# Sums over V ahead of both units' scores at the head of an even turn

## The chip, the cores and the metric

The kernel runs on one core of a Trainium2 chip. The metric is the device time of one execution in microseconds (us). TensorE (PE) multiplies matrices, VectorE (DVE), ScalarE (ACT) and GpSimd (POOL) work on elements, and SyncE (SP) issues the transfers. Each engine runs its instructions in the order in which the program lists them; between engines they wait for one another by semaphores.

## The reference

Top-k attention over 8 batches, 8 heads, 576 positions and a head width of 64, then a SwiGLU feed-forward block over the 4608 resulting rows of 512 (inner width 1536). In short:

```
scores = q @ k.T / 8                              # 576 x 576 for each batch and head
kth    = 32nd largest score of each row
attn   = softmax(scores where scores >= kth, else -1e9)
x      = (attn @ v), heads put side by side        # 4608 x 512
out    = (silu(x @ w_gate) * (x @ w_val)) @ w_out  # 4608 x 512
```

All of it is fp32.

## The kernel before, in words

**Units.** Attention is cut into units of one batch, one block of 128 query rows (`qt`) and one pair of heads (`hp`): 576 rows make four blocks of 128 and one of 64. A unit of a block of 128 is a full unit: two heads, 576 scores each for 128 rows. The last block of a batch gives half units: its 64 rows of both heads lie together on 128 partitions. A batch has 16 full units and then 4 half units; there are 160 units in all.

**Turns.** The main loop (L843) makes one turn for each unit `n`. The loop's body fixes the order of work by hand, and the end of the kernel (L912 to L925) ties each engine's instructions to that order. In turn `n`:

- VectorE selects the top 32 of unit `n` (`select`, L322: four rounds of MAX8, L334, with three MATCH_REPLACE8, L338, for each head).
- ScalarE turns unit `n-1` into exponentials (`weigh`, L354: a Prelu, L361, and an Exp with its sum, L366, for each head). From unit 32 on VectorE adds a small constant to the sums (L379), and it takes their reciprocals (L380, `normalize`). ScalarE (L384) and GpSimd (L386) then scale the two heads.
- TensorE transposes unit `n-2` (`turn`, L390: into PSUM tiles `etps`, L400), and ScalarE copies the result into the tile `et` (L401).
- At an even turn TensorE multiplies the transposed weights of units `n-4` and `n-3` by V (`values`, L411: 40 matmul records, L434, into one PSUM tile `av`), and ScalarE copies these sums into `xT`, the input of the feed-forward block (L450). That is "the sums over V of two units". `finish_units` (L820) calls this, and at the end of a batch's units it also starts the load of the next batch's V (`load_v`, L237).
- At an even turn TensorE makes the scores of units `n+1` and `n+2` (`scores`, L284). For a full unit these are four products into four PSUM tiles `s` (L314, eight records), each of which ScalarE copies with its scale into `sc` (L319); for a half unit two tiles (L300, L305). The generator stops once between the matmuls and the copies, so that a caller can place these apart. The second unit's copies come only after `weigh`, since the three buffers of `sc` allow no more.
- The feed-forward block runs in pieces in between (`piece`, L751; `feed`, L564): products with the weights (tile `f`, L578), gates on ScalarE and GpSimd (L611 to L619) and the output products (`y_ps` and `x_ps`, L644). A planner gives each turn a credit (`share`, L787), from the costs of its other work, and takes pieces while it lasts: two right after the head of the turn, one or two later, the rest at the end of the turn. Work that ScalarE and GpSimd still owe to pieces is put into two lists (`on_act`, `on_pool`) and written out at fixed places (`flush`).
- Now and then a turn also prepares keys and queries of a later pair of heads (`fetch`, `prep`: transposes into `kqps`, L267 and L260, and copies L263, L264 and L272).

**Buffers.** PSUM is in two pools: `ps_t` with five tiles (scores, `av`, `etps`, `kqps`), given out one after the other in a circle, and `ps_f` with three (products of the feed-forward block). A tile can be written again when the copy that reads its last contents is done.

**The place of the change** is the head of the turn:

```python
        flush(on_pool)
        if nxt:
            run(nxt.pop(0))           # scores of unit n+1, with their copies
        if valued(n):
            finish_units(valued(n))   # sums over V of units n-4 and n-3
        if nxt:
            next(nxt[0])              # matmuls of unit n+2's scores
        early[0]()
        if 0 <= n - 1 < NU:
            weigh(n - 1)
        if nxt:
            run(nxt.pop())            # copies of unit n+2's scores
```

Here `scored(n)` (L801) names the units to score: both at an even turn, none at an odd one (turns 0 and 1 score one each). `valued(n)` (L806) names the two units to sum, at even turns only.

Of the kernel before, what the change touches and what calls it, by code (L numbers as in the profile page):

```python
# [25 lines left out]
def kernel(  # L26
# [174 lines left out]
    def rounding(n):  # L201
        for _ in range(n):
            next(weight, None)
# [33 lines left out]
    def load_v(i):  # L237
        b, hp = pairs[i]
        h = slice(2 * hp, 2 * hp + 2)
        vt = slabs.tile([P, 2, J, D], FP32, tag="v", name="v")  # L240
        v_last = slabs.tile([R, 2, D], FP32, tag="vl", name="v_last")
        vl = vlast[i % NV]
        nc.sync.dma_start(
            vt[:].rearrange("p h j d -> p h (j d)"),
            v[b, h, 0:JP].rearrange("h (p j) d -> p h (j d)", j=J),
        )
        nc.sync.dma_start(v_last[:], v[b, h, JP:S].rearrange("h p d -> p h d"))
        for hh in range(2):
            o = hh * R
            nc.sync.dma_start(vl[o : o + R, o : o + R], v[b, 2 * hp + hh, JP:S])  # L250
        vs[i] = (vt, v_last, vl)
# [28 lines left out]
    def n_heads(qt):  # L280

        return 1 if qt == J else 2

    def scores(n):  # L284
        b, qt, hp = units[n]
        slab = preps[b * NHP + hp]
        sc = work.tile([P, 2 * S], FP32, tag="sc", name="sc", bufs=3)
        halves = [slice(0, D), slice(D, P)]
        half = S // 2

        def bank():
            return ps_t.tile([P, 512], FP32, tag="t", name="s")


        if qt == J:
            banks = [bank() for _ in range(2)]
            for i, ps in enumerate(banks):
                for d in halves:
                    k0 = R + i * half
                    nc.tensor.matmul(  # L300
                        ps[d, 0:half], slab[d, S + R : S + 2 * R], slab[d, k0 : k0 + half]
                    )
            yield
            for i, ps in enumerate(banks):
                nc.scalar.mul(sc[:, i * half : (i + 1) * half], ps[:, 0:half], scale)  # L305
        else:
            q0 = S + 2 * R + qt * P
            banks = []
            for i in range(2):
                for hh, d in enumerate(halves):  # L310
                    ps = bank()
                    banks.append((i + 2 * hh, ps))
                    k0 = (1 - hh) * R + i * half
                    nc.tensor.matmul(  # L314
                        ps[:, 0:half], slab[d, q0 : q0 + P], slab[d, k0 : k0 + half]
                    )
            yield
            for i, ps in banks:
                nc.scalar.mul(sc[:, i * half : (i + 1) * half], ps[:, 0:half], scale)  # L319
        state[n] = dict(sc=sc)  # L320

    def select(n):  # L322

        nh = n_heads(units[n][1])
        sc = state[n]["sc"]
        m = small.tile([P, 2, TOP_K], FP32, tag="m", name="m")
        heads = [slice(t * S, (t + 1) * S) for t in range(nh)]
        e = work.tile([P, 2 * S], FP32, tag="e", name="e", bufs=3)
        state[n] |= dict(m=m, e=e, heads=heads)
        cur = sc  # L330
        rounds = TOP_K // 8
        for r in range(rounds):
            for t, hs in enumerate(heads):
                nc.vector.max(m[:, t, 8 * r : 8 * r + 8], cur[:, hs])  # L334
                yield
            if r < rounds - 1:
                for t, hs in enumerate(heads):
                    nc.vector.match_replace(  # L338
                        e[:, hs], m[:, t, 8 * r : 8 * r + 8], cur[:, hs], LOWEST
                    )  # L340
                    yield
                cur = e

    def shift(n):

        st = state[n]
        m, nh = st["m"], len(st["heads"])
        bias = small.tile([P, 2], FP32, tag="bias", name="bias")
        nc.gpsimd.tensor_tensor(  # L349
            bias[:, 0:nh], m[:, 0:nh, TOP_K - 1], m[:, 0:nh, 0], ALU.subtract  # L350
        )
        st["bias"] = bias
# [21 lines left out]
    def normalize(n):  # L374
        st = state[n]
        tot, e, heads = st.pop("tot"), st["e"], st.pop("heads")
        nh = len(heads)
        for t in range(nh if n >= AHEAD else 0):
            nc.vector.tensor_scalar_add(tot[:, t : t + 1], tot[:, t : t + 1], EPS)  # L379
        nc.vector.reciprocal(tot[:, 0:nh], tot[:, 0:nh])  # L380
        yield
        for t, hs in enumerate(heads):
            if t == 0 and n >= 3 * NHP:
                nc.scalar.mul(e[:, hs], e[:, hs], tot[:, t : t + 1])  # L384
            else:
                nc.gpsimd.tensor_tensor(  # L386
                    e[:, hs], e[:, hs], tot[:, t : t + 1].to_broadcast([P, S]), ALU.mult
                )
# [83 lines left out]
    def flush(queue):  # L472
        while queue:
            queue.pop(0)()
# [303 lines left out]
    def fetch(n):  # L778

        b, qt, hp = units[n]  # L780
        i = b * NHP + hp
        if qt == 0:
            yield from prep(i)
        if qt == J and i + NHP < len(pairs):
            load(i + NHP)

    def share(n):  # L787


        others = 0.0  # L790
        costs = [(m, 0.7) for m in scored(n) + valued(n)] + [(n - TURN, 0.6)]
        for m, cost in costs:
            if m >= 0:
                others += cost * (0.5 if units[m][1] == J else 1)
        if units[n + 3][1] == 0:
            others += 0.6

        beside = 5.8 if n < AHEAD else 6.4
        return beside * n_heads(units[n][1]) / 2 - others

    def scored(n):  # L801

        ahead = [n + 1] if n < 2 else [] if n % 2 else [n + 1, n + 2]
        return [m for m in ahead if m < NU]

    def valued(n):  # L806

        behind = [] if n % 2 else [n - 4, n - 3]
        return [m for m in behind if 0 <= m < NU]

    def pieces(n):
        for _ in range(n):
            if credit[0] >= 1:
                credit[0] -= piece()

    def run(steps):
        for _ in steps:
            pass

    def finish_units(ns):  # L820
        values(ns)
        for n in ns:
            b, qt, hp = units[n]
            if qt == J and b + 1 < B:
                load_v((b + 1) * NHP + hp)
# [17 lines left out]
    for n in range(NU + 3):  # L843
        nh = n_heads(units[n][1]) if n < NU else 1
        topk = select(n) if n < NU else no
        norm = normalize(n - 1) if 0 <= n - 1 < NU else no
        nxt = [scores(m) for m in scored(n)]
        ahead = fetch(n + 3 if n else 2) if n + 3 < NU else no

        def dve(k, beside=True):  # L850

            for _ in range(k * nh):
                next(topk, None)
                due[0] += 5 / 6 if beside else 0
                if due[0] >= 1:
                    due[0] -= 1
                    rounding(1)

        if n >= NU - NHP:
            credit[0] = 8.0  # L860
        else:
            credit[0] = min(credit[0] + share(n), share(n) + 1)
        flush(on_act)
        if 0 <= n - 1 < NU:
            shift(n - 1)
        flush(on_pool)
        if nxt:
            run(nxt.pop(0))
        if valued(n):
            finish_units(valued(n))  # L870
        if nxt:
            next(nxt[0])
        early[0]()
# [3 lines that stand above are left out]
            run(nxt.pop())  # L877


        dve(2, beside=False)  # L880
        if n == 0:
            run(ahead)
            load(3)
            ahead = fetch(3)
        if n < NHP:
            load_v(n)
        pieces(2)
        flush(on_act)
        dve(1)
        dve(1)  # L890
        if 0 <= n - TURN < NU:
            run(turn(n - TURN))

        flush(on_pool)
        next(ahead, None)
        pieces(1)
        next(ahead, None)
        dve(1)
        pieces(1)
        if n < AHEAD:  # L900
            dve(1, beside=False)
        run(norm)
        dve(1 if n < AHEAD else 2, beside=False)
        run(topk)
        pieces(6)
# [50 lines left out]
```

## Time and profile before

| what | us |
|---|---|
| median of 3 runs | 1760.57 |
| lowest, highest run | 1758.68, 1762.17 |
| the profiled execution | 1759.77 |
| its span, first to last instruction | 1758.0 |
| TensorE busy in the span | 1679.6 |
| VectorE busy | 1476.5 |
| ScalarE busy | 1262.3 |
| GpSimd busy | 798.8 |

The mean granted clock of TensorE was 0.974 of full speed. Times in a timeline count from the span's start. A row of a timeline stands for consecutive records of one kind: start, length, engine, line, operation, output from inputs, shapes, their number, and in brackets how long the engine was idle before and what ended that. PE stands for matmuls, PEld for the loading of weights, which overlaps them. Matmuls are pipelined and their ends are modelled, so the distance between starts tells more than the ends do. The attention part ends at about 1690 us; after that only feed-forward work is left.

### The profile page before, as it was taken

What the parts mean: (1) busy time and instruction counts of PE and PEld (TensorE: products, weight loads), DVE (VectorE), ACT (ScalarE), POOL (GpSimd) and SP (SyncE); (2) the same over time, 40 slices, a digit from 0 to 9 for tenths busy, and PEclk for the clock granted to TensorE, in tenths of its full rate; (3) what the DMA queues carried; (4) which work ended last, traced back from release to release, by engine and by line L of the source; (5) the groups of instructions that cost most, each with busy time, mean ns of one, the idle gap of its engine ahead of it and who ended that gap; (6) DMA issues with size and microseconds to landing.
All of it is one profiled execution on the core that took longest, in us unless ns stands there. A gap on an engine that the chain in (4) does not pass through costs nothing.

```text
span 1758.0 us, 31754 instructions
## 1 busy us (share of the span) xinstructions
PE 1679.6 (96%) x11408; PEld 1404.5 (80%) x11408; DVE 1476.5 (84%) x3311; ACT 1262.3 (72%) x2901; POOL 798.8 (45%) x910
## 2 busy tenths in 40 slices
PE   5578999999999999999999999999999999999999
PEld 3468588787888788887888878887888878788887
DVE  6999899989889899898899898898988988898300
ACT  7899787777767686768776777777776777676431
POOL 4898534343353425352535334443444433535434
PEclk6698999999999999999999999999999999999999
DMA  7442120003000120002100020000300020000000
GB/s 200 138 120 86 29 68 1 13 2 83 15 13 1 28 70 1 13 12 59 28 13 1 14 70 27 1 13 19 78 2 13 1 57 15 13 1 13 1 13 12
DMA packets 109309, 59.72 MB, mean 34 GB/s; under 512 B 88544, under 2 KB 96992, under 8 KB 109152
## 3 DMA queue, kind: packets, MB, share of 16 engines
q1 hardware_dynamic: 108016, 57.37, 12.5%
q8 instruction: 90, 1.47, 0.4%
q14 instruction: 67, 0.55, 0.1%
q10 hardware_dynamic: 1136, 0.33, 0.1%
HBM read 48.23 MB, written 9.44 MB: 33 GB/s over the span
## 4 chain that ended last, share of the span: by engine, by line
PE 81%; DVE 8%; ACT 8%; POOL 1%; issue 1%; DMA 1%; SPq 0%; ACTq 0%; POOLq 0%
PE f L578 37%; PE av L434 9%; PE x_ps L644 9%; PE s L314 7%; PE y_ps L644 7%; PE etps L400 6%; DVE m L334 4%; DVE e L338 3%; PE f L494 3%; ACT e L366 2%; PE s L300 2%; PE kqps L267 1%; ACT e L361 1%; ACT et L401 1%; PE o_ps L546 1%
## 5 line engine op out<-in xcount | busy, mean ns | idle before, releaser
L334 DVE MAX8 m<-e 128x8 f32<-128x576 f32 x864 | 615.0, 748 | 3.1
L338 DVE MATCH_REPLACE8 e<-m,e 128x576 f32<-128x576 f32 x576 | 423.9, 743 | 0.0
L578 PE MATMUL f<-xT,wg 128*128 128x256 f32 x1536 | 355.0, 381 | 0.0
L578 PE MATMUL f<-xT,wv 128*128 128x256 f32 x1536 | 353.9, 380 | 0.0
L578 PEld LDWEIGHTS f<-xT,wg 128*128 128x128 f32 x1536 | 287.7, 190 | 45.7 <-issue 8.4
L578 PEld LDWEIGHTS f<-xT,wv 128*128 128x128 f32 x1536 | 286.8, 190 | 42.7 <-issue 5.5
L614 POOL TENSOR_TENSOR h<-h,half_g 128x512 f32<-128x512 f32 x96 | 122.5, 1276 | 352.7 <-ACT h L613 336.8
L366 ACT ACTIVATE e<-e,bias 128x576 f32<-128x576 f32 x288 | 221.2, 776 | 34.1 <-POOL bias L349 30.9
L400 PE MATMUL etps<-ident,e 128*128 128x128 f32 (+1 forms) x1312 | 182.9, 281 | 46.7 <-POOL e L386 19.3
L400 PEld LDWEIGHTS etps<-ident,e 128*128 128x128 f32 (+1 forms) x1312 | 154.3, 143 | 76.9 <-POOL e L386 25.3
L338 DVE MATCH_REPLACE8 e<-m,sc 128x576 f32<-128x576 f32 x288 | 211.9, 742 | 0.0
L361 ACT ACTIVATE e<-sc,m 128x576 f32<-128x576 f32 x288 | 211.3, 786 | 0.0
L334 DVE MAX8 m<-sc 128x8 f32<-128x576 f32 x288 | 203.3, 743 | 7.5 <-ACT sc L319 7.5
L319 ACT ACTIVATE sc<-s 128x288 f32<-128x288 f32 x512 | 167.5, 414 | 53.4 <-PE s L314 53.0
L619 POOL TENSOR_TENSOR h<-h,val 128x512 f32<-128x512 f32 x96 | 122.5, 1276 | 178.5 <-ACT val L618 166.0
L386 POOL TENSOR_TENSOR e<-e,tot 128x576 f32<-128x576 f32 x140 | 160.8, 1152 | 87.4 <-DVE tot L380 76.2
L401 ACT COPY et<-etps 128x512 f32<-128x512 f32 (+1 forms) x448 | 183.4, 489 | 12.2 <-PE etps L400 11.7
L314 PE MATMUL s<-kqT 64*128 64x288 f32 x1024 | 171.3, 444 | 16.4 <-ACT et L401 8.3
L379 DVE TENSOR_SCALAR tot<-tot 128x1 f32<-128x1 f32 x228 | 29.4, 146 | 172.0 <-ACT e L366 171.9
L434 PE MATMUL av<-et,v 128*64 128x128 f32 (+1 forms) x2560 | 158.7, 267 | 0.0
L384 ACT ACTIVATE e<-e,tot 128x576 f32<-128x576 f32 x148 | 118.5, 801 | 46.5 <-DVE tot L380 46.2
L314 PEld LDWEIGHTS s<-kqT 64*128 64x128 f32 x1024 | 95.1, 191 | 62.2 <-issue 24.0
(85 smaller groups left out, 2279.0 us busy)
## 6 DMA issues: line engine op xcount, KB each, us to landing
v<-in_v_dram SPq DMA_DIRECT2D x32, 256.0 KB, 3.4
kq_in<-in_k_dram SPq DMA_DIRECT2D x63, 128.0 KB, 2.9
kq_in<-in_q_dram SPq DMA_DIRECT2D x63, 128.0 KB, 3.3
w<-in_moe_w_gate_dram SPq DMA_DIRECT2D x12, 512.0 KB, 3.9
w<-in_moe_w_val_dram SPq DMA_DIRECT2D x12, 512.0 KB, 3.7
w<-in_moe_w_out_dram SPq DMA_DIRECT2D x12, 512.0 KB, 3.6
out_dram<-o SPq DMA_DIRECT2D x38, 128.0 KB, 2.4
out_dram<-o SPq DMA_DIRECT2D x16, 256.0 KB, 2.4
```

What stands on the lines that cost most here:

```text
L314: nc.tensor.matmul(ps[:, 0:half], slab[d, q0 : q0 + P], slab[d, k0 : k0 + half])
L319: nc.scalar.mul(sc[:, i * half : (i + 1) * half], ps[:, 0:half], scale)
L334: nc.vector.max(m[:, t, 8 * r : 8 * r + 8], cur[:, hs])
L338: nc.vector.match_replace(e[:, hs], m[:, t, 8 * r : 8 * r + 8], cur[:, hs], LOWEST)
L361: nc.scalar.activation(e[:, hs], sc[:, hs], AF.Prelu, bias=m[:, t, TOP_K - 1 : TOP_K], scale=-1.0, alpha=SMALL,)
L366: nc.scalar.activation(e[:, hs], e[:, hs], AF.Exp, bias=bias[:, t : t + 1], scale=-1.0 / SMALL, accum_out=tot[:, t : t + 1],)
L386: nc.gpsimd.tensor_tensor(e[:, hs], e[:, hs], tot[:, t : t + 1].to_broadcast([P, S]), ALU.mult)
L400: nc.tensor.transpose(ps[0:kl, c * P : (c + 1) * P], e[:, k0 : k0 + kl], ident[:])
L401: nc.scalar.copy(et[0:kl, c0 : c0 + cn, :], ps[0:kl, 0 : cn * P].rearrange("p (c j) -> p c j", c=cn),)
L434: nc.tensor.matmul(av[d, i, 0:ql], weights_, moving, start=c == (0 if last else J), stop=c == (J if last else J - 1),)
L578: nc.tensor.matmul(ps[:, i, :], w[:, kc, m * P : (m + 1) * P], x[:, kc, :], start=(kc == 0), stop=(kc == KC - 1),)
L644: nc.tensor.matmul(ps, lhsT, T[i][m], start=m == 0, stop=m == MQ - 1)
```

## The change

At the head of a turn the two blocks change places: `finish_units` now comes ahead of the scores of unit `n+1`. On TensorE an even turn's head so has the 40 matmuls of `av` first and then the scores of both units, one after the other. On ScalarE the copy of `av` (L450) comes ahead of the four copies of unit `n+1`'s scores (L319). The PSUM tiles of `ps_t` are given out in that new order. Nothing is added or left out; odd turns and turns without both kinds of work keep their order.

```diff
@@ -864,10 +864,10 @@
         if 0 <= n - 1 < NU:
             shift(n - 1)
         flush(on_pool)
+        if valued(n):
+            finish_units(valued(n))
         if nxt:
             run(nxt.pop(0))
-        if valued(n):
-            finish_units(valued(n))
         if nxt:
             next(nxt[0])
         early[0]()
```

## The prediction

> **What bounds the kernel now.** I read the page first: its busy line, then windows by stage, to see where TensorE is full.
>
> ```profile
> PE 1679.6 (96%) x11408; PEld 1404.5 (80%) x11408; DVE 1476.5 (84%) x3311; ACT 1262.3 (72%) x2901; POOL 798.8 (45%) x910
> 0.00:200.00 200.00, 147.97 (x999) 114.85 (x999) 182.59 (x382) 167.36 (x373) 147.38 (x136) 0.81 0.43 121
> 400.00:1600.00 1200.00, 1189.18 (x8065) 998.76 (x8067) 1074.57 (x2450) 879.32 (x2032) 502.71 (x605) 1.00 0.10 24
> ```
>
> (Windows: stretch, length, busy us of PE, PEld, DVE, ACT, POOL, then clock and DMA.) From 400 to 1600 us TensorE is 99% busy at full clock, so its order of work sets the end; in the first 200 us it has slack and VectorE (91%) sets the pace. "Busy" hides short pauses between matmuls, and the change acts on exactly those. So I next asked who waits for whom.
>
> ```profile
> DVE tot L379 <- ACT e L366: 171.9, 107, 13.1
> PE etps L400 <- ACT sc L319: 19.3, 13, 3.9
> PE s L314 <- ACT et L401: 8.3, 3, 3.5
> PE s L314 <- ACT sc L319: 6.8, 3, 5.9
> ```
>
> (us, times, longest.) TensorE hardly waits; VectorE waits for ScalarE's exponentials 107 times, so it follows TensorE through ScalarE and has room. Last, the timeline of a head of an even turn with two full units, TensorE first, then ScalarE:
>
> ```profile
> 890.96 1.89 PE L578 MATMUL f<-xT,wg 128*128 128x256 f32 x8
> 892.78 1.24 PE L314 MATMUL s<-kqT 64*128 64x288 f32 x8
> 893.95 0.44 PE L434 MATMUL av<-et,vlast 128*64 128x128 f32 x4
> ...
> 896.29 1.24 PE L314 MATMUL s<-kqT 64*128 64x288 f32 x8
> 897.46 1.35 PE L578 MATMUL f<-xT,wg 128*128 128x256 f32 x5
> ...
> 893.57 1.32 ACT L319 ACTIVATE sc<-s 128x288 f32<-128x288 f32 x4 [1.82 <-PE s L314]
> 896.40 0.37 ACT L450 COPY xT<-av 128x256 f32<-128x256 f32 x1 [1.52 <-PE av L434]
> 896.67 1.45 ACT L361 ACTIVATE e<-sc,m 128x576 f32<-128x576 f32 x2
> ```
>
> By starts: first scores 1.17 us, sums over V 2.34, second scores 1.17; a head of 4.68 us from s to f. ScalarE stands idle before the scores' copies and again before the copy of the sums: it has room here.
>
> One place shows what scores cost when their banks come free one by one from ScalarE's copies:
>
> ```profile
> 348.63 1.33 ACT L319 ACTIVATE sc<-s 128x288 f32<-128x288 f32 x4
> 349.11 1.65 PE L314 MATMUL s<-kqT 64*128 64x288 f32 x8 [0.19 <-ACT sc L319]
> 350.69 0.48 PE L578 MATMUL f<-xT,wg 128*128 128x256 f32 x1
> ```
>
> There s to f is 1.58 us instead of 1.17. The four copies last 1.33 with single records of 0.43, so they follow each other at 0.30; the first ends at 349.06 and the matmul starts at 349.11, 0.05 later.
>
> **What the skill says.** The Trainium skill, "TensorEngine Tiling (Array Packing)", Key Properties: changing the tiling mode, not only the tile, drains TensorE. The trace agrees: s is 64\*128, av 128\*64, f 128\*128. Eight f take 1.82 us ahead of s (890.96 to 892.78), where eight at the pitch of 0.216 (24 of L578 in 5.18 in the chain) take 1.73: 0.09 to leave. Single records within the s row start 0.35, 0.24, 0.24 apart and the next row 0.34 after the last: 0.10 to enter, 0.10 to leave. "TensorE: Matmul & The Clock Gate", Part 3, The mechanism: matmuls start in program order, so one that waits for a bank holds what is behind it; the stretched s row at 349.11 fits that.
>
> **The change, part by part.** No instruction is added or removed. At an even turn the 40 matmuls of av and ScalarE's copy L450 go ahead of s of unit n+1; the second s row then follows the first directly.
>
> (a) *One change of mode less.* Before: f, s, av, s, f; after: f, av, s, s, f. The pair "out of av, into s" stays, "out of s, into av" goes: about 0.10 + 0.05 (first step in av 0.16 instead of 0.11), and "f to s" becomes "f to av", 0.05 cheaper. Gain 0.20 us a head if nothing waits.
>
> (b) *A wait for banks.* Tag t has five banks, given out in turn. Before, the order is s ABCD, av E, s ABCD, and 2.34 us of av cover the four copies that free A to D. After, it is av A, s BCDE, s ABCD: of the second row, bank 1 needs the copy of av, banks 2, 3, 4 the first three copies of the row just before, and no work lies between. With the sums first, s begins 2.33 after the head. The first copy starts 0.79 after it (893.57 minus 892.78), the third ends 0.79 + 2 x 0.29 + 0.42 = 1.79 after it, and its bank's matmul starts at 1.84 instead of 1.57. In the row at 349.11 the last bank was freed three copies after the first, at 0.90, and f came at 1.58: 0.68 later. So f follows at 1.84 + 0.68 = 2.52, and the head is 2.33 + 2.52 = 4.85 us against 4.68: **+0.17 net**, (a) included. ScalarE must be free by 2.4 for this; in every full head after 410 us its earlier work ends at most 2.0 after the head.
>
> (c) *How many.* I sorted the heads by time. After 410 us 42 have two full units ahead (FF): 36 of them at 4.68 (or 4.09, where the sums are of half units; after, 1.75 + 2.52 = 4.27): 36 x 0.17 = +6.1. The other six, first in their batch, take 4.35, 4.43, 4.42, 4.24, 4.69, 4.24 since s waits for a copy of et or kqT; with the sums in front that wait is covered: 6 x 4.27 - 26.37 = -0.75. Where a half unit takes part the second row needs two banks, or its banks are old: no wait. Six heads half-half: -0.2 each. Six full-half: mode changes from 64\*128 to 64\*64, so between 0 and -0.2, I take -0.1. Five half-full: transposes follow at once and wait for a copy of the second scores (819.07, 0.65 us); L361 comes 0.18 earlier because two copies follow 0.75 after s at 2.33, against 3.84: -0.18. Together -2.7. Sum after 410 us: +2.65.
>
> (d) *200 to 410 us*: four plain FF heads +0.7, one at 224.85 with a covered wait -0.44, two where ScalarE was late anyway 0, four mixed about -0.65: -0.4. *Before 200 us* VectorE sets the pace: 0, bounded by -1 and +2 (two heads whose sums now fill a wait for et, against five where the transposes wait for L319).
>
> (e) *ScalarE.* In an FF head L361 (weigh) starts after four copies: 2.33 + 0.79 + 4 x 0.29 = 4.28 instead of 3.89, 0.4 us late. Behind it queue L366, the second scores' L319, gates and et copies. Late next: VectorE at L379, which waits 0.4 longer but is ahead of TensorE there; transposes of this turn, at 8.23 after the head, need two L319 copies that now end near 7.6 and 7.9 against a need of about 8.9 (second bank group): covered by the two pieces of f, 3.5 us. Without them it would cost up to 0.4 an FF head. In the odd turn the transposes at 907.18 need POOL's L386, done at 904.77: covered by 2.4. Where DMAs go: load_v only follows av, which is now earlier; SP issues the same list in the same order, POOL too.
>
> Sum: +2.65 - 0.4 + 0 = about **+2.2 us** on the profiled execution, whose span is 1758.0 and own time 1759.8: 1762.0. The median of the runs shown is 0.8 above that execution: **1762.8 us**.
>
> **Rivals.**
> 1. *Only the saved mode change counts* (banks come free in time): 70 heads after 200 us x 0.20, -14 us, 1746 or 1747. For it: ScalarE is idle at the head. Against it: the first copy can't start before 0.79, longer than the 0.24 a matmul steps. Chance 0.08.
> 2. *The late weigh reaches TensorE* (the other side): place, the transposes of the same turn behind L319, or those of the next turn behind L386. Price 0.4 an FF head on top of (b): about 46 FF heads after 200 us x 0.4 = +18, 1780; it decides once the slack above (about 1.0 and 2.4 us) is used up in most heads. For it: 13 waits of L400 for L319 already, 19.3 us. Against it: only 6 us of these lie after 200 us. Chance 0.10.
> 3. *A dearer bank wait*: matmuls in order also hold the first bank's second half, or ScalarE starts the copies late: 0.30 to 0.40 a head, 46 x 0.15 to 0.2 = +7 to +9 on top: 1770. For it: the 1.58 row. Chance 0.24.
> 4. *Main case*, 1762.8, own range 1759 to 1767. Chance 0.58.
>
> **How the numbers follow.** 0.2% is 3.5 us, about what a measurement of this kernel can tell from no change. Of the main case a quarter lies above 1764.1, since (b) is uncertain by 0.05 on 46 heads, 2.3 us, and the start by 2; 0.42 stays within, 0.15 slower. Rival 2 and nearly all of 3 are slower (0.33), rival 1 faster; 0.01 of rival 3 is within, 0.01 of the main case faster. Faster 0.09, same 0.43, slower 0.48. The range 1758 to 1772 takes in the main case and rival 3 and leaves out rivals 1 and 2.
>
> **What would show it.** The chain and timeline after should show f, av, s x16, f; the two s rows together about 2.5 us; a new wait "PE s L314 <- ACT sc L319" at FF heads, or a gap of TensorE's weight loads there; L379 waiting some 15 to 20 us longer; fewer waits of s for L401. I am wrong if the s rows together take 2.14 (no bank wait), if transposes wait for L319 in FF turns, or if windows before 200 us lose more than 2 us.

## The result, and the profile after

The changed kernel takes 1768.17 us (median of 5 runs, 1767.79 to 1769.47) against 1760.57: a ratio of 1.0047, interval 1.0032 to 1.0061. It is slower by about 8 us. The profiled execution took 1767.96 us with a span of 1766.2 (before: 1758.0), so its span accounts for the loss: +8.2 us.

The page's busy line, and the two stretches by windows, with the columns of those shown of before:

```profile
PE 1686.3 (95%) x11408; PEld 1433.6 (81%) x11408; DVE 1475.7 (84%) x3311; ACT 1264.5 (72%) x2901; POOL 797.9 (45%) x910
0.00:200.00 200.00, 149.43 (x1032) 119.15 (x1034) 182.67 (x384) 167.46 (x373) 147.13 (x136) 0.83 0.43 121
400.00:1600.00 1200.00, 1187.54 (x7995) 1015.12 (x7995) 1065.77 (x2429) 878.94 (x2027) 496.58 (x598) 1.00 0.10 24
```

In the first 200 us TensorE got 33 matmuls further than before (1032 against 999). From 400 to 1600 us it did 70 fewer (7995 against 8065) while just as "busy". So the loss lies in the middle of the kernel, spread thin, and not in idle time that the page shows. The weight loads give it away: PEld is busy 16 us longer in that stretch, for fewer loads.

The list of waits of the changed kernel (total us, times, longest):

```profile
DVE tot L379 <- ACT e L366: 180.5, 108, 13.1
PE etps L400 <- ACT sc L319: 20.9, 14, 3.7
PE s L314 <- ACT sc L319: 5.4, 2, 5.0
```

TensorE's listed wait of scores for the copies of scores did not grow (6.8 before), though the change makes the second row of scores wait at every head with two full units; the waits of scores for L401 (8.3) are gone, and the sums, which now come first, wait 4.6 us for L401. The same head as in the prediction, in the timeline of the changed kernel, TensorE and then ScalarE:

```profile
895.87 0.44 PE L434 MATMUL av<-et,vlast 128*64 128x128 f32 x4
...
898.20 2.60 PE L314 MATMUL s<-kqT 64*128 64x288 f32 x16
900.73 2.00 PE L578 MATMUL f<-xT,wg 128*128 128x256 f32 x8
...
898.32 0.37 ACT L450 COPY xT<-av 128x256 f32<-128x256 f32 x1 [3.48 <-PE av L434]
898.99 1.32 ACT L319 ACTIVATE sc<-s 128x288 f32<-128x288 f32 x4 [0.30 <-PE s L314]
900.16 1.46 ACT L361 ACTIVATE e<-sc,m 128x576 f32<-128x576 f32 x2
```

The sums take 2.33 us, as before (2.34); the two rows of scores now take 2.53 (898.20 to 900.73) where they took 1.17 each, 2.34. The head is 4.86 us long here (895.87 to 900.73) against 4.68; over all heads of this kind the mean is 4.87. The sixteen products are one unbroken row in the record: no wait is listed, because the pauses sit between matmuls whose recorded lengths overlap. They show when the records are taken one by one. These are the second and the third copy of the first row's scores, and weight loads of the second row:

```profile
899.29 0.40 ACT L319 ACTIVATE sc<-s 128x288 f32<-128x288 f32 x1
899.58 0.42 ACT L319 ACTIVATE sc<-s 128x288 f32<-128x288 f32 x1
...
899.75 0.29 PEld L314 LDWEIGHTS s<-kqT 64*128 64x128 f32 x2
900.05 0.29 PEld L314 LDWEIGHTS s<-kqT 64*128 64x128 f32 x2
```

The copies end at 899.70 and 900.00, and each time the loads for the next tile begin 0.05 us later. The first copy ends at 899.40, and the loads that need its tile begin at 899.45. So the second row moves at the pace of the copies, 0.30 us a tile, where its products start 0.24 apart in a free row. Over the whole kernel the pauses show in the groups of weight loads, before and after:

```profile
L314 PEld LDWEIGHTS s<-kqT 64*128 64x128 f32 x1024 | 95.1, 191 | 62.2 <-issue 24.0 <-ACT et L401 11.7 <-ACT sc L319 8.6
```

```profile
L314 PEld LDWEIGHTS s<-kqT 64*128 64x128 f32 x1024 | 122.9, 191 | 39.1 <-issue 11.4 <-ACT sc L319 7.1 <-ACT kqT L272 3.5
```

The same 1024 loads of the same mean length fill 27.8 us more: loads that overlapped each other now stand apart, because the products behind them are held back one by one. It is the wait that does this and not the new order: with that order and two tiles a unit, where no row waits for the one before it (experiment 2), the loads fill 94.7 us.

Put side by side head by head (from the starts of TensorE's rows; sums over heads of a kind), the +8.2 us of span fall into these places. FF stands for a head with two full units to score; a full-half head scores a full unit and then a half one, a half-full head the other way round, a half-half head two half units.

| where | us |
|---|---|
| up to the head at 199 us | -1.4 |
| 199 to 417 us (0.9 of it one head at half clock) | +2.0 |
| after 417 us: 36 plain FF heads, 0.19 each | +6.9 |
| the six FF heads that come first in their batch | -0.6 |
| heads with half units, with the stretch up to the next head of these | about 0 |
| four stretches between heads (+0.20, +0.23, +1.70, +0.35) | +2.5 |
| the last two heads, after 1684 us | -1.2 |

### The profile page after: what moved, and what is told of

Same layout as the page of the kernel before. It is cut to its first block, busy times and chain, and to the rows that moved or that the text cites. A ratio compares the mean times of both kernels' runs of the same rounds, so it can differ in the third digit from the quotient of the medians.

```text
span 1766.2 us, 31757 instructions
## 1 busy us (share of the span) xinstructions
PE 1686.3 (95%) x11408; PEld 1433.6 (81%) x11408; DVE 1475.7 (84%) x3311; ACT 1264.5 (72%) x2901; POOL 797.9 (45%) x910
## 4 chain that ended last, share of the span: by engine, by line
PE 82%; ACT 8%; DVE 6%; POOL 2%; issue 1%; DMA 0%; SPq 0%; ACTq 0%; POOLq 0%
PE f L578 36%; PE av L434 10%; PE x_ps L644 9%; PE s L314 7%; PE etps L400 6%; PE y_ps L644 6%; PE f L494 3%; DVE m L334 3%; DVE e L338 3%; ACT e L366 2%; PE s L300 2%; PE kqps L267 1%; ACT e L361 1%; ACT sc L319 1%; PE o_ps L546 1%
## 5 line engine op out<-in xcount | busy, mean ns | idle before, releaser
L366 ACT ACTIVATE e<-e,bias 128x576 f32<-128x576 f32 x288 | 222.7, 787 | 35.8 <-POOL bias L349 32.6
L361 ACT ACTIVATE e<-sc,m 128x576 f32<-128x576 f32 x288 | 212.6, 798 | 0.0
L401 ACT COPY et<-etps 128x512 f32<-128x512 f32 (+1 forms) x448 | 184.5, 497 | 7.8 <-PE etps L400 7.1
L319 ACT ACTIVATE sc<-s 128x288 f32<-128x288 f32 x512 | 168.4, 419 | 20.3 <-PE s L314 20.3
L314 PE MATMUL s<-kqT 64*128 64x288 f32 x1024 | 173.8, 447 | 8.8 <-ACT sc L319 5.4
L379 DVE TENSOR_SCALAR tot<-tot 128x1 f32<-128x1 f32 x228 | 29.4, 145 | 180.8 <-ACT e L366 180.5
L314 PEld LDWEIGHTS s<-kqT 64*128 64x128 f32 x1024 | 122.9, 191 | 39.1 <-issue 11.4
```

The source lines that it names most:

```text
L314: nc.tensor.matmul(ps[:, 0:half], slab[d, q0 : q0 + P], slab[d, k0 : k0 + half])
L361: nc.scalar.activation(e[:, hs], sc[:, hs], AF.Prelu, bias=m[:, t, TOP_K - 1 : TOP_K], scale=-1.0, alpha=SMALL,)
L366: nc.scalar.activation(e[:, hs], e[:, hs], AF.Exp, bias=bias[:, t : t + 1], scale=-1.0 / SMALL, accum_out=tot[:, t : t + 1],)
L401: nc.scalar.copy(et[0:kl, c0 : c0 + cn, :], ps[0:kl, 0 : cn * P].rearrange("p (c j) -> p c j", c=cn),)
```

## The experiments

**Theories.** *Bank*: the loss is the wait for PSUM tiles (the prediction calls them banks) inside the two rows of scores, less one change of mode. *Late*: the loss is that the exponentials (L361, L366) come later on ScalarE, and what follows them reaches TensorE. A third question is what the two parts of the bank theory are worth one by one.

**1 and 2. The bank wait taken away, in both orders.** A full unit's four products go into two tiles instead of four, so five tiles hold two rows of scores and no product waits for a copy of the row just before. A tile holds 512 columns and two products of 288 overlap in 64, so 64 of a head's 576 scores are overwritten in these kernels; sizes and numbers of instructions stay. The first has the order of before, the second that of the change.

```diff
+            two = [bank() for _ in range(2)]
             for i in range(2):
                 for hh, d in enumerate(halves):
-                    ps = bank()
 ...
+                    ps, p0 = two[hh], i * (512 - half)
 ...
```

Order of before:

> Control for two_bank_after: the order of the kernel before, but a full unit's four score products go into two PSUM tiles instead of four (256 of each tile's columns are free of overlap; 64 of a head's 576 score columns are overwritten by the second product before they are copied, so the scores there are not the reference's). Same number and size of matmuls and copies. Bank theory and late-ScalarE theory agree here: no bank was short in this order, so the time stays at 1760 us within 3, with full heads at 4.68 us.

Changed order:

> The changed order with two tiles for a full unit's scores (64 score columns of each head overwritten, as in two_bank_before): av, s, s then take five tiles in all, so the second row of scores needs no tile of the first. Bank theory: the wait of about 0.39 us goes and the saved change of mode of 0.20 us stays; full heads take about 4.47 us against 4.68, and the time is some 10 us below two_bank_before (49 full heads after 200 us x 0.20), about 1750. Late-ScalarE theory (what costs is that exponentials start later): here they start later still, as the first copy waits for both products of a tile, so the time stays at or above that of the changed kernel, 1768 or more.

Measured: 1753.94 (ratio 0.996, 0.9947 to 0.9973) and 1752.39 (0.9955, 0.9942 to 0.9967). The plain FF head is 4.68 us in the first, as in the kernel before, and 4.48 in the second. From the timeline of the second (its line numbers are one higher, as the edit adds a line):

```profile
887.62 2.21 PE L315 MATMUL s<-kqT 64*128 64x288 f32 x16
889.77 1.99 PE L579 MATMUL f<-xT,wg 128*128 128x256 f32 x8
...
888.90 1.32 ACT L320 ACTIVATE sc<-s 128x288 f32<-128x288 f32 x4 [0.78 <-PE s L315]
890.08 1.46 ACT L362 ACTIVATE e<-sc,m 128x576 f32<-128x576 f32 x2
```

The rows of scores take 2.15 (887.62 to 889.77) where the changed kernel needs 2.53. So the price of a plain FF head is split: 4.68 to 4.48, **the mode change saves 0.20**; 4.48 to 4.87, **the bank wait costs 0.39**. The first kernel missed its expectation: it is 6 us faster than before, and of the 8.5 us that its span is shorter 6.5 are gained ahead of the head at 368 us; why is left open. The second one gained only 1.5 us over the first, not the 9 that the 46 FF heads after 200 us would give: its heads gain 0.20 each, but stretches between heads lose 0.6 to 2.7 us in nine places after 200 us. Its exponentials start 4.79 after the head (890.08 minus 885.29) instead of 3.89. That pointed to the late theory.

**3. Both rows of scores first, then the sums.**

```diff
         if nxt:
             run(nxt.pop(0))
+        if nxt:
+            next(nxt[0])
         if valued(n):
             finish_units(valued(n))
-        if nxt:
-            next(nxt[0])
         early[0]()
```

> Both units' scores first, the sums over V last: the same single change of mode saved and the same short supply of tiles (s ABCD, s EABC), but the copy of the sums and with it the exponentials come about 1 us later than in the changed kernel. Bank theory: full heads at 4.87 us as in the changed kernel, time 1768 within 2. Late-ScalarE theory: about 1 us more at each of some 50 full heads, 1800 or more, with transposes waiting for score copies.

Measured: 1840.79 (1.0463, 1.0446 to 1.0479). It has the bank wait, with most FF heads at 4.87 as in the change, and the copy of the sums comes last, with the exponentials queued behind it. Some 32 us are lost before 417 us. After that its FF heads lose 17.1 us together, more than the 0.19 each, probably since some have no sums in front to cover ScalarE's earlier work; half-full heads lose 6.6, and the stretches between heads some 25. So a late ScalarE can be far dearer than the bank wait.

**4 and 5. The two kinds of heads apart.** The sums go first only where both scored units are full, or only where a half unit is scored (`any(... == J)` in place of `all(... != J)`).

```diff
+        sums_first = all(units[m][1] != J for m in scored(n))
+        if valued(n) and sums_first:
+            finish_units(valued(n))
         if nxt:
             run(nxt.pop(0))
-        if valued(n):
+        if valued(n) and not sums_first:
             finish_units(valued(n))
```

Full heads only:

> The sums go ahead of the scores only at heads whose two units to score are both full; the other heads keep the order of before. Bank theory: all of the loss is here (49 such heads after 200 us, 46 of them without an old wait to cover, x 0.19 = 8 to 9 us), 1768 to 1769 us. If the heads with half units carry a share of the loss, this falls clearly below 1768.

Half heads only:

> The sums go ahead of the scores only at heads where at least one of the two units to score is a half unit; full heads keep the order of before. Bank theory: no bank is short there; half-half heads save 0.15 us each, which the next wait for a copy takes back: 1760 within 2, not to be told from the kernel before. If those heads carry a share of the loss, 1763 or more.

Measured: 1767.88 (1.0042, 1.0028 to 1.0056) and 1760.41 (1.0005, 0.9997 to 1.0014). The heads with two full units account for the loss, and for the heads with half units no effect can be told. In the first, FF heads after 405 us lose 6.23 us and the stretches between heads only 0.7. In the second the six half-half heads gain 0.88 us, and the stretches in front of half-full heads give 0.8 back; the stretch in front of the last half-half head loses 0.36.

**6 and 7. The change and the kernel before once more**, without an edit, to see what one kernel differs by from profile to profile.

> The changed kernel once more, for a second trace. Bank theory: again 0.19 us more in every plain full head. If the 3.4 us of half clock at 225 and at 1529 us of the first trace come by chance of where a wait falls, they sit elsewhere or are missing here, and the span differs by 1 to 2 us for it; if the new order causes them, they recur at the same two places.

> The kernel before once more, for a second trace, to see how much two executions of one program differ: plain full heads at 4.68 us again; stretches of half clock after 330 us should be missing or sit at other places than in the changed kernel; the time 1760 within 2.

Measured: 1768.56 (1.0047, 1.0033 to 1.006) and 1760.49 (1.0, 0.999 to 1.0009). The profiles of before differ by 1.4 us in the first 200 us and are the same head by head afterwards. So the -1.4 of the change in the start can't be told from chance. The changed kernel's slow head at 224 us (5.58 us, with TensorE's clock at half for 3.4 us) took 4.29 in the repetition: chance as well. Row by row, the table above reads +0.3, +0.7, +6.9, -0.6, about 0, +2.7 and 0 for the repetition (span +9.9), against the same profile of before: the rows in the middle come back, while the first, the second and the last differ by 1.2 to 1.7 us between two profiles of one kernel.

**8 and 9. A later ScalarE alone.** The order of before, with ScalarE's copy of the sums made two or four times; TensorE's order and tiles stay. In the traces the exponentials come 0.41 and 1.21 us later at most plain FF heads (4.30 and 5.10 after the head, against 3.89), more than the 0.3 and 0.8 of the expectations, since the copies start 0.40 apart. So with two copies they come as late after the head as in the changed kernel. What is queued behind them on ScalarE comes later too.

```diff
-            nc.scalar.copy(
-                xT[kb][:, hps, at - kb * BLK : at - kb * BLK + n_c],
-                av[:, 0 : len(ns), at - c0 : at - c0 + n_c],
-            )
+            for _ in range(2):
+                nc.scalar.copy(
+                    xT[kb][:, hps, at - kb * BLK : at - kb * BLK + n_c],
+                    av[:, 0 : len(ns), at - c0 : at - c0 + n_c],
+                )
```

Two times:

> The order of the kernel before, with ScalarE's copy of the sums over V made twice. Nothing changes on TensorE; the exponentials start about 0.3 us later at each even turn (a copy takes 0.27 us from start to start), a little less than in the changed kernel (0.4). This prices the late exponentials alone. Bank theory: heads stay at 4.68 us and lateness costs next to nothing, 1760 to 1762. Late-ScalarE theory: most of the changed kernel's 8 us appears here, 1765 or more.

Four times:

> The same with the copy of the sums made four times: exponentials about 0.8 us late, near the 1.0 us of scores_first and the lateness of two_bank_after, with TensorE's heads as before. If lateness has a threshold between 0.4 and 1.0 us, as scores_first (1841 us) suggests, this costs several times what late_1 costs: 1775 or more. If scores_first lost its 80 us to its heads alone, this stays under 1766.

Measured: 1774.89 (1.0093, 1.0079 to 1.0106) and 1814.3 (1.0311, 1.0296 to 1.0327). Against runs of before taken beside them (median 1759.26), a delay of 0.41 us on ScalarE, at 72% busy, costs 15.6 us, and 1.21 us costs 55. From the trace with two copies, ScalarE at the head at 900.95:

```profile
904.57 0.78 ACT L451 COPY xT<-av 128x256 f32<-128x256 f32 x2 [1.52 <-PE av L434]
905.24 1.44 ACT L361 ACTIVATE e<-sc,m 128x576 f32<-128x576 f32 x2
```

Every FF head after 405 us keeps its length there. Of the span's 15.1 us, 5.8 are lost before 417 us, 2.5 of them in one head that ran in part at half clock. After 405 us 8.1 us are lost between heads, 4.4 of these in the ten stretches just before and just behind half-full heads. There TensorE waits twice for ScalarE. The timelines of before, of the change and of the kernel with two copies, at the same half-full head:

```profile
812.89 0.33 PE L260 MATMUL kqps<-ident,kq_last 128*128 128x128 f32 x1 [0.60 <-ACT et L401]
...
819.07 0.30 PE L400 MATMUL etps<-ident,e 128*64 128x128 f32 x1 [0.65 <-ACT sc L319]
```

```profile
815.69 0.33 PE L260 MATMUL kqps<-ident,kq_last 128*128 128x128 f32 x1 [0.77 <-ACT et L401]
...
821.90 0.30 PE L400 MATMUL etps<-ident,e 128*64 128x128 f32 x1 [0.67 <-ACT sc L319]
```

```profile
820.61 0.33 PE L260 MATMUL kqps<-ident,kq_last 128*128 128x128 f32 x1 [1.00 <-ACT et L401]
...
827.20 0.30 PE L400 MATMUL etps<-ident,e 128*64 128x128 f32 x1 [1.05 <-ACT sc L319]
```

With the copy made twice both waits grow by 0.40. In the change the second hardly moves and the first grows by 0.17, which is what the half-half head ahead of it had gained (0.15): TensorE comes earlier to a ScalarE that is no earlier. At these turns, then, ScalarE sets the pace (the exponentials and the copies queued behind them), not TensorE's order. Which of its instructions counts most is not separated here.

**10. The changed order in two tiles, with the exponentials early.** As experiment 2, with the same 64 columns overwritten, but on ScalarE the exponentials go right behind the copy of the sums, ahead of both units' score copies: they start 2.7 us after the head. The edit against the changed kernel, without that of the tiles:

```diff
-        if nxt:
-            run(nxt.pop(0))
-        if nxt:
-            next(nxt[0])
+        for made in nxt:
+            next(made)
         early[0]()
         if 0 <= n - 1 < NU:
             weigh(n - 1)
-        if nxt:
-            run(nxt.pop())
+        for made in nxt:
+            run(made)
```

> two_bank_after (64 score columns of each head overwritten), but ScalarE makes the exponentials ahead of the first unit's score copies, so that they start about 1.2 us earlier than in the kernel before, not later. In two tiles the scores of the second unit need none of the first. If two_bank_after kept its 0.20 us a full head and gave it back through late exponentials, this kernel keeps the gain: some 10 us below two_bank_before, about 1743. If the gain was lost otherwise, it stays near 1752.

Measured: 1744.85 (0.992, 0.9907 to 0.9934). Against experiment 2 that is 7.5 us for a move on ScalarE alone (6.4 when each is taken against the runs of before beside it).

**11. The order of before, with the exponentials early.** Nothing changes on TensorE and in PSUM, and the whole result is computed: the exponentials move ahead of the copy of the sums, into the time in which ScalarE waits for them.

```diff
         if nxt:
             run(nxt.pop(0))
+        if 0 <= n - 1 < NU:
+            weigh(n - 1)
         if valued(n):
             finish_units(valued(n))
         if nxt:
             next(nxt[0])
         early[0]()
-        if 0 <= n - 1 < NU:
-            weigh(n - 1)
         if nxt:
             run(nxt.pop())
```

> TensorE keeps the order of before (s, av, s); on ScalarE the exponentials of L361 and L366 move ahead of the copy of the sums (L450), into the time in which ScalarE waits for av, so they start about 1.8 us earlier at even turns. If exponentials in time are what the few waits between heads hang on (as the runs with the copy made two and four times say), heads stay at 4.68 us, the waits of transposes and of L260 for ScalarE shrink, and the time is 1745 to 1755. If the wait only moves, since the copy of the sums now ends later and the feed-forward products (L578) or the second scores' copies wait for it, 1760 or more.

Measured: 1747.32 us (1744.05 to 1748.27; ratio 0.9923, 0.991 to 0.9937). It beats both kernels. Its ScalarE at a plain FF head (head at 889.14), and then TensorE at the half-full head of above:

```profile
891.10 1.46 ACT L361 ACTIVATE e<-sc,m 128x576 f32<-128x576 f32 x2
...
893.95 0.38 ACT L450 COPY xT<-av 128x256 f32<-128x256 f32 x1
```

```profile
810.06 0.33 PE L260 MATMUL kqps<-ident,kq_last 128*128 128x128 f32 x1 [0.31 <-ACT et L401]
...
815.12 0.77 PE L400 MATMUL etps<-ident,e 128*128 128x128 f32 x5
```

The exponentials start 1.96 after the head instead of 3.89. The sums' copy is 1.2 us later, and no wait of TensorE for it shows behind 400 us but one of 1.1 us. Plain FF heads keep 4.68. At the half-full head the wait of 0.60 is 0.31 and that of 0.65 is gone. In the waits of TensorE after 400 us, the transposes' for L319 are 4.3 us before, 4.3 in the change, 6.7 with two copies and none here. In the first 200 us this kernel is 2.5 us behind before; the gain is made later. The five half-full heads after 405 us and the stretches on both sides of them bring 7.2 us, the part behind 1684 us brings 3.9, and single stretches the rest.

## Why the prediction was right or wrong, point by point

The time lies in the range given and on the side with the larger chance (slower by over 0.2%, 0.48); the likeliest value, 1762.8, was 5.4 us too low. That the range holds is partly luck: the main case by itself ended at 1767, and the range reached 1772 only for rival 3, which did not come.

*Step (a), the mode change, 0.20 a head: right*, shown by experiments 1 and 2 (4.68 to 4.48).

*Step (b), the bank wait: right in mechanism and nearly in size.* Predicted: scores of 2.52 us, head 4.85, +0.17. Measured: 2.53, 4.87, +0.19 at every plain FF head, of which the wait is 0.39; tile by tile, loads follow the copies by the 0.05 us that the prediction read. Rival 3's dearer wait (0.30 to 0.40 net) did not come, although the time is near its 1770; rival 1 falls with (b).

*Step (c), how many: the count was right and its mixed heads failed.* 36 heads at 0.19 are +6.9, predicted 6.1. First in the batch: -0.64, predicted -0.75. The mixed heads were to bring -2.7 and brought about 0. This is the step of the sum that failed most clearly. Full-half heads, taken at -0.1, stayed at 4.62. Half-half heads gained 0.15 (predicted 0.2), given back in the next stretch as the longer wait of L260. Half-full heads were to gain 0.18, since L361 was to come 0.18 earlier. It came 0.04 later, 3.88 after the head (819.83 in the changed kernel) against 3.84: I let two copies of a half unit follow in 0.75, but its two tiles are made one after the other, and ScalarE waits for the second:

```profile
819.04 0.90 ACT L305 ACTIVATE sc<-s 128x288 f32<-128x288 f32 x2 [0.26 <-PE s L300]
819.83 0.77 ACT L361 ACTIVATE e<-sc,m 128x576 f32<-128x576 f32 x1
```

*Step (d), the start.* 200 to 410 us: predicted -0.4, measured +2.0 (0.7 in the repetition), of which 0.9 is the head at half clock and 0.8 four FF heads at 0.19; the covered wait at 225 us lies under that head, and in the repetition it brought 0.42 (4.71 to 4.29; predicted 0.44). The four mixed heads, taken at -0.65, brought nothing here either. Before 200 us: -1.4, inside what one kernel differs by.

*Step (e), ScalarE 0.4 late at nothing: right for the turns it was worked out for, and short of a rule.* Exponentials do come 0.40 later in FF heads (4.29 after the head), but TensorE's own turn is 0.19 longer, so they are late by 0.2 in effect. Half-full heads, where experiment 8 lost some 0.8 each, were spared, since L361 came only 0.04 later there. The waits of transposes for L319 after 400 us are the same (4.3 us, six times). Rival 2 so did not come as stated. Still its mechanism is at the door: three stretches between FF heads lost 2.1 us (+0.20, +0.23, +1.70) and one more 0.35 (it also came in experiment 5, so it goes with the heads with half units), which the step had put at nothing. The large one has a wait for GpSimd's scaling that grew by 0.18: the 2.4 us of cover that the step found at one turn are not there at this one. The timelines of before, of the change, and of experiment 4 with the sums first at FF heads alone:

```profile
1522.58 0.77 PE L400 MATMUL etps<-ident,e 128*128 128x128 f32 x5 [2.13 <-POOL e L386]
```

```profile
1529.69 1.33 PE L400 MATMUL etps<-ident,e 128*128 128x128 f32 x5 [2.31 <-POOL e L386]
```

```profile
1529.37 0.77 PE L400 MATMUL etps<-ident,e 128*128 128x128 f32 x5 [2.31 <-POOL e L386]
```

The other 1.5 us are TensorE's clock, in windows of the changed kernel (the last three columns are clock, DMA share, GB/s):

```profile
1526.00:1529.40 3.40, 1.37 (x9) 0.98 (x7) 3.40 (x8) 0.00 (x0) 3.40 (x5) 1.00 0.00 0
1529.40:1532.80 3.40, 3.11 (x10) 2.76 (x11) 2.38 (x9) 2.98 (x9) 1.41 (x4) 0.50 0.00 0
```

For 3.4 us it ran at half, at the end of the longer wait. The same came in the repetition of the change and in experiments 2 and 10 near this place, and in neither profile of before. But the longer wait alone does not do it. In experiment 4 the wait is 2.31 us too, in experiment 8 it is 2.44, and the clock stayed full in both; in experiment 4 this stretch lost 0.19 and not 1.70. So these 1.5 us can't be booked as a price of the longer wait, and what decides them stays open.

*What would show it.* The order, the length of the rows and the missing waits for L401 came as written. The wait "PE s L314 <- ACT sc L319" did not show at FF heads; the weight loads did, though as longer busy time and not as the gap that was named (their listed idle time fell from 62.2 to 39.1 us). L379 waits 8.6 us longer, not 15 to 20: VectorE's work is unchanged (1476.5 and 1475.7 us busy), so it can't stand idle for longer than the kernel grows, and I should have seen that.

In sum, against the +2.2 predicted for the span the +8.2 measured has 2.7 more from the mixed heads, 2.5 from stretches between heads, 2.4 from 200 to 410 us and 0.9 from FF heads, less 1.4 in the start and 1.2 at the end. The first and the last of the four additions are shown by experiments 4 and 5 and the head-by-head comparison; those from 200 to 410 us are partly chance, as are the two that are taken off, and of the stretches' 2.5 us 1.5 are the drop in clock. What is safe is the 0.19 at 36 heads, which all three profiles with the sums first at FF heads show.

## What to carry to other kernels

When two blocks change places, list the order in which PSUM tiles are handed out before and after: a row of products that follows directly on the row that filled the same tiles waits for its copies, and that wait may show in no list, only in single records, as weight loads spread out and as a row that is longer from start to start. Look on the other engine, too, for what sits behind a copy: here moving TensorE's blocks was worth -0.20 and +0.39 us a head, while moving ScalarE's exponentials into time it spent waiting was worth 12 us in all (experiment 11). Before a gain is booked for TensorE arriving earlier, check that the engine it waits for next is also earlier.

## What the runs showed of the hardware that was not expected

- A row of 16 products of which some wait for tiles is shown as one unbroken row; the 0.39 us of waiting appear in the starts of single loads (899.45, 899.75 and 900.05, each 0.05 behind a copy) and in the weight loads' busy time (95.1 to 122.9 us, mean 191 ns in both).
- TensorE's clock fell to 0.50 for 3.40 us (1529.40 to 1532.80) at the end of a wait of 2.31 us, and not behind one of 2.13 in the kernel before, nor behind 2.31 in experiment 4 and 2.44 in experiment 8. The half-clock stretches of the changed kernel's trace at 225.522, 321.095 and 1529.413 start 28 and 354 times 3.413 us apart, so they lie on a grid. Whether the place of a wait on this grid matters besides its length is not tested here.
- ScalarE, busy 72% of the span, has places without room: 0.41 us more at an even turn cost 15.6 us in all, 1.21 us cost 55.
